# A block of linear attention and a gated MLP on one core: residual of the down phase added in DRAM, two more products by seven, W_down sums moved, the last tile in three parts, a new order

## The chip, the cores and the metric

The kernel runs on one core of a Trainium2 chip. The core has a matrix engine (PE, with its weight loads PEld), a vector engine (DVE), a scalar engine (ACT), GpSimd (POOL) and SyncE (SP), which run their own instruction streams and meet only at semaphores. Matrix products land in PSUM, eight banks of 128 x 512 fp32. SP, ACT and POOL start DMA transfers, which 16 DMA engines carry out. The metric is the device time of one launch in microseconds, the median of several runs: 732.98 us before (732.70 to 734.86, three runs).

## The reference

An adaLN-conditioned block on 2048 rows of width 1024: linear attention with 32 heads, then a gated MLP with 3584 inner columns. Inputs, weights and output are bfloat16.

```python
mod = (silu(c) @ w_mod)                  # six rows of 1024: sa, ca, ga, sb, cb, gb
h = layernorm(x) * (1 + ca) + sa
x = x + ga * A(h, wqkv, wo)              # linear attention
h = layernorm(x) * (1 + cb) + sb
x = x + gb * (gelu(h @ w_gate) * (h @ w_up) @ w_down)
```

The change lies mostly in the last product, `@ w_down`, and in `x + gb * (...)`, the residual.

## The kernel before

**Stages.** `start_phase` and `kvq_phase` make the attention's K, V and Q products; `merge_phase` folds the per-head matrices and Wo into one weight; `wo_phase` multiplies by it, writes the sum x2 (the first residual) to `x2_scr` in DRAM and its normalised form to `xh_scr`. Then the MLP runs in two groups g = 0 and 1 of 1024 rows each: `gate_up(g)` (gate and up products, 14 units of about 12 us) and `down_out(g)` (the product with W_down, gate, residual and store).

**Products by seven.** Large products are cut into 2 x 2 blocks and done with seven block products in place of eight (Winograd's form of Strassen's scheme). In `down_out` the seven products of the outer level are called b11, b21, t0, t1, b22, t2 and t3, by the quarter of W_down, or the sum of quarters, that they read. Each is a product of 512 rows by 1792 by 512 columns. It is done in one of two ways:

- `plain(name, A, out, start)`: W_down's operand is loaded in one DMA of 1792 KB; for each of four row tiles q, 14 matmuls with 512 columns, so 56 matmuls.
- `nested(name, A, S, keep, out)`: by seven once more. Seven operands of 448 KB are loaded; each of the steps g1 to g7 is 14 matmuls with 256 columns, so 98 matmuls. It needs four sums of A's blocks on DVE (`sub_sums`, into the tiles `S`), four sums of W_down's blocks made beforehand (in `u_scr` for b21, b22 and t0, in `v_scr` for b11 and t2), and copies of partial results from PSUM on ACT (`fcopy`).

Before the change, nested are b21, t0 and b22 in both groups, and b11 and t2 in group 1; plain are b11, t1, t2, t3 in group 0 and t1, t3 in group 1.

**W_down's sums.** t0 to t3 are made in DRAM or through SBUF: `wd_moves` lets POOL issue copies and accumulating DMAs (28 in all) from W_down into `t_scr`; `wd_sums` makes, on DVE, t1, t3 and the block sums of `u_scr` in `merge_phase` and `gate_up(0)`. `wd_later(c)`, called in the units 0 to 6 of `gate_up(1)`, loads two rows of b11 and of t2, makes eight sums on DVE and stores them to `v_scr` by POOL.

**Residual.** `rest(half, nh)` loads a 512 KB block of x2 into SBUF on SP's queue; the output functions (`c11_out`, `u2_out`, `c12_out`, `finish`, `c22_quads`, `c21_last`) multiply by the gate row `gbrow`, add that block on DVE, and `store` sends 256 KB blocks to the output, by POOL's queue in group 0 and by ACT's in group 1. All DVE additions of this kind go through the helper `tt_op`, so they all carry line 789.

**The end.** In group 1 the last product is t3 (`plain` with `c21_last`), row tiles in the order 0 to 3; the last tile is done in two parts of 256 columns, which lie in the same PSUM bank.

**Order.** Nothing is issued as it is called: `Plan` records every operation with its dependences and estimated cost, sweeps the list forwards and backwards to give each a due time (`order`), and `refine` then moves the instructions of each engine by hand-fixed shifts from the tables `SHIFTS`, one table for each of PE, DVE, ACT, POOL and SP. Each engine issues in its own fixed order.

**Memory.** SBUF is laid out by hand. `W_AT[g][name]` gives the slots of 3.5 KB per partition that the operands of W_down use. The tiles `x2_ring` at 207 to 219 KB take the x blocks that `wo_tile` adds in `wo_phase`; `early_r`, `early_t`, `early_u` at the same place serve `wd_sums(0)` and `wd_sums(1)`.

```python
        def store(xt, half, nh, lo, hi, c=slice(0, NW)):
            r = (2 * g + half) * TG
            (ac if last else gp).dma_start(
                out=o_dram[r + lo * P:r + hi * P, nh * NW:(nh + 1) * NW][:, c].rearrange("(q p) n -> p q n", p=P),
                in_=xt[:, lo:hi, c])
```

Of the kernel before, what the change touches and what calls it, by code (L numbers as in the profile page):

```python
# [509 lines left out]
def kernel(  # L510
# [839 lines left out]
    def wd_moves(seen_of, n):  # L1350


        if not wd_todo:
            return
# [185 lines left out]
    def merge_phase(stages):  # L1540
# [4 lines left out]
        for i, stage in enumerate(stages):  # L1545
# [20 lines left out]
            if i >= 6:  # L1566
                wp_step(wp.pop(0))
# [636 lines left out]
```

## Time and profile before

The profiled execution took 735.55 us by the clock of the runs; its span, from the first to the last instruction, is 733.5 us, so 2.05 us lie around it. The median of the runs is 2.57 us lower than this execution. Shares are of the span.

| | before |
|---|---|
| median of the runs | 732.98 us |
| profiled execution, its span | 735.55 us, 733.5 us |
| PE busy | 723.0 us (99%), 4352 matmuls |
| DVE busy | 652.4 us (89%), 1470 instructions |
| ACT busy | 455.6 us (62%) |
| POOL busy | 101.5 us (14%) |
| mean granted TensorE clock | 0.995 |
| DMA | 159.26 MB, mean 217 GB/s |

By stage (start and end in us of the span): start, K, V and Q 0 to about 150; merge about 150 to 186; Wo products 186 to 240; `gate_up(0)` 240 to about 404; `down_out(0)` about 404 to 480; `gate_up(1)` about 480 to 648; `down_out(1)` about 648 to the end. The stages overlap by some us, since an engine begins the next as soon as its operands are there.

A profile line names the source line, the engine, the operation, what it writes and reads (`mem` is the SBUF tile, `psum` the PSUM tile, `us`, `vs`, `ts`, `x2s` the DRAM scratch tensors), how many there were, and then busy time and the mean duration of one. A mean duration of a matmul includes its way through the array; the spacing of matmuls that follow each other is read from a block of them instead.

### The profile page before, as it was taken

To read this page: it belongs to the slowest core of one execution; us is meant where nothing else is said; L and a number is where in the kernel's file an instruction comes from. 1 tells how busy PE (TensorE), PEld (TensorE's weight loads), DVE (VectorE), ACT (ScalarE), POOL (GpSimd) and SP (SyncE) were. 2 spreads that over 40 slices of the span, in tenths; PEclk is the share of its full clock that TensorE was granted. 3 is DMA by queue.
4 is the path that set the end of the run, shared out by engine and by line. 5 is a ranking of instruction groups with operands and counts; after the bars stand their busy time and mean duration, and the time that the engine had idled before them with its cause. 6 is when DMAs were issued, how large, how long until landed. Compare 5 with 4: busy or idle time off the path is not lost.

```text
span 733.5 us, 12117 instructions
## 1 busy us (share of the span) xinstructions
PE 723.0 (99%) x4352; PEld 405.7 (55%) x4365; DVE 652.4 (89%) x1470; ACT 455.6 (62%) x829; POOL 101.5 (14%) x174
## 2 busy tenths in 40 slices
PE   7999999999999999999999999999999999999997
PEld 3444545444444555555555677445555555568774
DVE  5699988797699999998998698978898999999998
ACT  4485656579687799999877722027676776743110
POOL 2143616010031014120200000010000100000000
PEclk8999999999999999999999999999999999999999
DMA  9868659988999777765776999554343544489982
GB/s 310 293 195 231 178 130 164 292 304 248 285 241 256 255 242 214 236 213 187 245 203 189 266 315 286 190 173 162 121 133 126 188 157 140 141 234 314 268 271 87
DMA packets 160988, 159.26 MB, mean 217 GB/s; under 512 B 34208, under 2 KB 140448, under 8 KB 160288
## 3 DMA queue, kind: packets, MB, share of 16 engines
q1 hardware_dynamic: 143568, 122.30, 55.6%
q0 software_dynamic: 14848, 33.82, 15.3%
q10 hardware_dynamic: 2512, 2.36, 1.0%
q8 instruction: 34, 0.56, 0.3%
q14 instruction: 26, 0.21, 0.1%
HBM read 122.42 MB, written 36.04 MB: 216 GB/s over the span
## 4 chain that ended last, share of the span: by engine, by line
PE 91%; ACT 3%; DMA 2%; DVE 2%; issue 1%; POOL 1%; SPq 0%; DVEq 0%; ACTq 0%
PE psum L1716 33%; PE psum L1977 12%; PE psum L1727 11%; PE psum L1932 10%; PE psum L1157 8%; PE psum L1227 5%; PE psum L1598 3%; PE psum L1534 3%; PE psum L1256 2%; PE psum L924 2%; DVE mem L789 1%; DMA mem<-in_A_x_dram 1%; DMA mem<-in_w_mod_dram 1%; PE psum L1271 1%; ACT mem L1317 0%
## 5 line engine op out<-in xcount | busy, mean ns | idle before, releaser
L789 DVE TENSOR_TENSOR mem<-mem 128x256 f16<-128x256 f16 (+12 forms) x855 | 377.9, 484 | 17.9 <-ACT mem L1094 4.6
L1716 PE MATMUL psum<-mem 128*128 128x512 f16 x1144 | 274.3, 379 | 0.1
L1094 ACT ACTIVATE mem<-psum 128x512 f32<-128x512 f32 (+3 forms) x318 | 165.0, 552 | 138.3 <-DVE mem L789 38.2
L789 DVE TENSOR_TENSOR mem<-psum,mem 128x512 f16<-128x512 f32 (+5 forms) x213 | 159.3, 756 | 34.3 <-ACT mem L1094 5.6
L1716 PEld LDWEIGHTS <-mem 128*128 128x128 f16 (+1 forms) x1144 | 111.8, 98 | 101.8 <-issue 0.3
L1727 PE MATMUL psum<-mem 128*128 128x256 f16 x742 | 107.4, 272 | 0.0
L1727 PEld LDWEIGHTS <-mem 128*128 128x128 f16 (+1 forms) x742 | 72.4, 98 | 43.1 <-issue 0.8
L1977 PE MATMUL psum<-mem 128*128 128x256 f16 (+1 forms) x784 | 88.2, 273 | 0.0
L1977 PEld LDWEIGHTS <-mem 128*128 128x128 f16 x784 | 76.7, 98 | 11.9
L1932 PE MATMUL psum<-mem 128*128 128x512 f16 (+2 forms) x348 | 75.2, 370 | 0.6 <-DVE mem L789 0.5
L1157 PE MATMUL psum<-mem 128*128 128x512 f16 (+1 forms) x274 | 62.2, 379 | 0.3
L1932 PEld LDWEIGHTS <-mem 128*128 128x128 f16 x350 | 34.2, 98 | 36.0 <-issue 0.7
L789 DVE TENSOR_TENSOR psum<-psum,mem 128x256 f32<-128x256 f32 x106 | 44.6, 427 | 8.7 <-ACT mem L1094 8.3
L1227 PE MATMUL psum<-mem 128*128 128x512 f16 x224 | 51.7, 379 | 0.0
L1772 ACT ACTIVATE psum<-psum 128x512 f32<-128x512 f32 x56 | 32.7, 586 | 30.4 <-DVE mem L789 21.9
L1157 PEld LDWEIGHTS <-mem 128*128 128x128 f16 x280 | 27.2, 98 | 31.6 <-DVE mem L1053 0.2
L1791 ACT ACTIVATE mem<-psum 128x512 f16<-128x512 f32 x56 | 33.1, 598 | 9.5 <-PE psum L1716 9.2
L1227 PEld LDWEIGHTS <-mem 128*128 128x128 f16 (+1 forms) x224 | 21.6, 98 | 25.3 <-issue 0.6
L1801 ACT ACTIVATE mem<-mem 128x512 f16<-128x512 f16 x56 | 34.7, 629 | 0.0
L1256 PE MATMUL psum<-mem 128*128 128x512 bf16 x123 | 29.0, 380 | 1.4 <-DVE mem L1029 0.8
L1335 POOL DMA_DIRECT2D ts<-in_B_w_down_dram x28 | 27.6, 1179 | 5.3 <-DMA ts<-in_B_w_down_dram 5.2
L1534 PE MATMUL psum<-mem 128*128 128x512 f16 x128 | 28.3, 379 | 0.0
(144 smaller groups left out, 574.6 us busy)
## 6 DMA issues: line engine op xcount, KB each, us to landing
mem<-in_B_w_gate_dram SPq DMA_DIRECT2D x14, 1024.0 KB, 5.3
mem<-in_B_w_up_dram SPq DMA_DIRECT2D x14, 1024.0 KB, 6.3
mem<-in_w_mod_dram SPq DMA_DIRECT2D x24, 512.0 KB, 6.8
mem<-us SPq DMA_DIRECT2D x24, 448.0 KB, 6.8
mem<-ts SPq DMA_DIRECT2D x5, 1792.0 KB, 6.7
ts<-in_B_w_down_dram POOLq DMA_DIRECT2D x28, 256.0 KB, 4.8
mem<-in_B_w_down_dram SPq DMA_DIRECT2D x15, 448.0 KB, 6.9
mem<-in_A_x_dram SPq DMA_DIRECT2D x23, 256.0 KB, 5.4
```

What stands on the lines that cost most here:

```text
L789: ve.tensor_tensor(out=out, in0=a, in1=b, op=op)
L1094: ac.activation(out=t, in_=ps, func=AF.Copy)
L1157: te.matmul(ps, lhsT=A[:, k, i * P:(i + 1) * P], rhs=B[:, k, :], start=(start and k == 0), stop=(k == KH - 1), skip_group_check=True)
L1227: te.matmul(o, lhsT=W[:, k, (j0 + i) * P:(j0 + i + 1) * P], rhs=h_form(a, k), start=(start and k == 0), stop=(k == KH - 1), skip_group_che ...
L1256: te.matmul(ps, lhsT=hr1[b][:, k, tl * P:(tl + 1) * P], rhs=Wk[:, k, n * NW:(n + 1) * NW], start=(k == 0), stop=(k == KD - 1))
L1534: te.matmul(psw[:, half, :], lhsT=pqT[b][:, g, tl * P:(tl + 1) * P], rhs=Wp[:, g, half * NW:(half + 1) * NW], start=(g == 0), stop=(g == K ...
L1716: te.matmul(ps, lhsT=a[:, k, e, :], rhs=b[:, k, :], start=(start and k == 0), stop=(k == KH - 1), skip_group_check=True)
L1727: te.matmul(ps, lhsT=self.x[a][:, k, :], rhs=self.y[y][:, k, :], start=(start and k == 0), stop=(k == KH // 2 - 1), skip_group_check=True)
L1791: ac.activation(out=o, in_=ps, func=AF.Gelu_apprx_tanh)
L1801: ac.activation(out=o, in_=o, func=AF.Gelu_apprx_tanh)
L1932: te.matmul(psm[:, q, c], lhsT=A[:, i, q * P:(q + 1) * P], rhs=wt[:, i, c], start=(start and i == 0), stop=(i == NPR - 1), skip_group_chec ...
L1977: te.matmul(ps[:, q, :], lhsT=a[:, k, q * P:(q + 1) * P], rhs=y[:, k, :], start=(start and q == 0 and k == 0), stop=(k == NPR // 2 - 1), s ...
```

## The change

1. **Residual.** `rest` and the DVE additions of x2 go, in all of group 0 and in half 0 of group 1. A new `added(half, nh)` gives a tile of the gated product in fp16, and its `send` adds 256 KB of it onto `x2_scr` in DRAM with an accumulating DMA on POOL's queue. When a half (512 rows) has been sent whole, one DMA copies its 1 MB from `x2_scr` to the output. Half 1 of group 1 stays as it was: loaded, added on DVE, stored by ACT's queue.
2. **Two more products by seven.** b11 in group 0 and t1 in group 1 go from `plain` to `nested`. With them come four sums of A11 each, the output functions `p1_quads` (now in both groups) and `u2_quads` (new), new tiles (`sub_c`), new slots in `W_AT`, and another interleaving of the steps (for example n1[5] and n1[6] behind n2[0] and n2[1]). In group 1 the copies that seed PSUM banks 0 to 3 move from `p1_quads` to `u2_quads`.
3. **W_down's sums.** `v_scr` holds sums for b11, t2 and now t1. Those of b11 are made in `merge_phase` (`wd_first`, stages 4 to 10) through SBUF tiles at 207 to 215 KB. Those of t2 and t1 are made wholly in DRAM: 16 copies and accumulating DMAs of 448 KB, two in each of the units 1 to 8 of `gate_up(1)`. `wd_later`'s loads, DVE sums and stores go.
4. **The last tile.** t3 of group 1 runs its row tiles in the order 2, 3, 0, 1; the last is done in three parts of 256, 128 and 128 columns, the second and third in banks 2 and 3, into which ACT copies the partial sums first.
5. **Order.** All five tables of `SHIFTS` are new. PE has 4463 instructions in them (4365 before), DVE 1429 (1457), ACT 810 (804), POOL 184 (153), SP 225 (226).

```diff
...
+    f32_ring.i = 2
...
-    wdv_rings = {"b11": Ring(207, [2, NW], BF16, 2), "t2": Ring(211, [2, NW], F16, 2)}
-    wdw_ring = Ring(215, [2, 4, HB], F16, 1)
+    first_r, first_v = Ring(207, [2, NW], BF16, 2), Ring(211, [4, HB], F16, 2)
...
-    sub_c = [at(a, [NPR // 2, HB], F16) for a in (207, 210.5, 214, 203)]
+    sub_c = [[at(a, [NPR // 2, HB], F16) for a in o] for o in ((215, 166, 170, 203), (207, 210.5, 214, 203))]
...
-    def wd_later(c):
...
+    def wd_first(c):
+
+        raw, v = first_r(), first_v()
+        plan.ahead = 60000
+        sy.dma_start(out=raw, in_=wd_full["b11"][:, 2 * c:2 * c + 2, :])
+        plan.ahead = 14000
+        q11, q12, q21, q22 = (raw[:, e, h * HB:(h + 1) * HB] for e in range(2) for h in range(2))
+        o0, o1, o2, o3 = (v[:, f, :] for f in range(4))
+        for out, a, b in ((o0, q11, q12), (o2, q12, q22), (o1, o0, q22), (o3, o1, q21)):
+            tt_op(out, a, b, ALU.add)
+        gp.dma_start(out=v_scr[:, c, 0], in_=v)
+
+    def wd_later():
...
+            todo.append([(o0, w[:, 0, 0], 0), (o2, w[:, 0, 1], 0), (o0, w[:, 0, 1], 1), (o2, w[:, 1, 1], 1),
+                         (o1, o0, 0), (o1, w[:, 1, 1], 1), (o3, o1, 0), (o3, w[:, 1, 0], 1)])
...
+            if 4 <= i < 4 + NPR // 2:
+                wd_first(i - 4)
...
-            if g and n < NPR // 2:
-                fill += wd_later(n)
+            if g and n == 0:
+                wd_todo.extend(wd_later())
+            if g and n:
+                wd_moves(w["s1"][:, 0, 0, 0:1], 2)
...
-    W_AT = [{"b11": 0, "b21": (4, 5, 6, 7, 8, 9, 10), "t0": (11, 12, 13, 0, 1, 2, 3), "t1": 4,
-             "b22": (14, 11, 12, 13, 8, 9, 10), "t2": 0, "t3": 11},
+    W_AT = [{"b11": (1, 2, 3, 4, 0, 5, 6), "b21": (7, 8, 9, 10, 11, 12, 13), "t0": (1, 2, 3, 4, 0, 5, 6), "t1": 11,
+             "b22": (7, 8, 9, 10, 4, 5, 6), "t2": 0, "t3": 11},
...
-             "t1": 11, "b22": (7, 8, 9, 0, 1, 2, 3), "t2": (4, 15, 16, 17, 18, 5, 10), "t3": 11}]
+             "t1": (11, 12, 13, 14, 7, 8, 9), "b22": (0, 1, 2, 3, 4, 15, 16),
+             "t2": (17, 18, 5, 6, 11, 12, 13), "t3": 7}]
...
+        def added(half, nh):
+
+            xt = acc_ring()
+
+            def send(lo, hi):
+                gp.dma_start(
+                    out=x2_scr[2 * g + half][lo * P:hi * P, nh * NW:(nh + 1) * NW].rearrange("(q p) n -> p q n", p=P),
+                    in_=xt[:, lo:hi], accum_op=ALU.add)
+                sent[half] += hi - lo
+                if sent[half] == 2 * TT:
+                    r = (2 * g + half) * TG
+                    gp.dma_start(out=o_dram[r:r + TG, :], in_=x2_scr[2 * g + half])
+            return xt, send
...
+            for q in (2, 3, 0, 1) if end else range(TT):
+                parts = [(0, HB, q), (HB, 3 * P, 2), (3 * P, NW, 3)] if end and q == 1 else [(0, NW, q)]
+                for lo, hi, b in parts:
+                    c = slice(lo, hi)
+                    if b != q:
+                        steps.append(lambda c=c, b=b, q=q: ac.activation(out=psm[:, b, c], in_=psm[:, q, c], func=AF.Copy))
...
-        def u2_out(xt):
-            def out(q, ps, c):
-                t = w12[:, q, :]
-                d = p5v[:, q, :] if last else t
-                tt_op(d, p5v[:, q, :], ps, ALU.subtract)
-                tt_op(t, d, gbrow[:, NW:D], ALU.mult)
-                tt_op(t, t, xt[:, q, :], ALU.add)
-            return out
...
+        def u2_out(q, ps, c):
+            t = w12[:, q, :]
+            tt_op(t, p5v[:, q, :], ps, ALU.subtract)
+            tt_op(t, t, gbrow[:, NW:D], ALU.mult)
+
+        def u2_quads(r, c, ps, sb, op):
+            u = quad(p1v, r, c)
+            if sb is not None:
+                tt_op(sb, ps, sb, op)
+                ps = sb
+            tt_op(u, ps, u, ALU.add)
+            if (r, c) in ((1, 0), (0, 1)):
+                rows = slice(2 * r, 2 * r + 2)
+                for q in (2 * r, 2 * r + 1):
+                    ac.activation(out=psm[:, q, :], in_=p1v[:, q, :], func=AF.Copy)
+                tt_op(p5v[:, rows], p5v[:, rows], p1v[:, rows], ALU.subtract)
+                tt_op(w12[:, rows], p5v[:, rows], gbrow[:, None, NW:D].to_broadcast((P, 2, NW)), ALU.mult)
...
-        if last:
-            sub_sums(A11, sub_c[:3], sub_c[3], [slice(0, 4), slice(4, NPR // 2 - 1), slice(NPR // 2 - 1, NPR // 2)])
-            run(*nested("b11", A11, sub_c[:3], sub_c[3], p1_quads))
-        else:
-            run(*plain("b11", A11, p1_out, True))
+        sub_sums(A11, S[:3], S[3], [slice(0, 4), slice(4, NPR // 2 - 1), slice(NPR // 2 - 1, NPR // 2)])
+        n1 = nested("b11", A11, S[:3], S[3], p1_quads)
+        run(*n1[:5])
...
+        if last:
+            sub_sums(A11, S[:3], None, [slice(0, NPR // 2)])
+            n6 = nested("t1", A11, S[:3], None, u2_quads)
+            run(n6[0], n5[5], n6[1], n5[6], *n6[2:5])
...
-            run(*plain("t3", A22, c21_last(x1), False))
+            m8 = plain("t3", A22, c21_last(x1), False)
+            run(m8[0], n7[5], m8[2], n7[6], m8[1], *m8[3:])
...
```

More of the change, by code (lines that the diff above doesn't have):

```diff
@@ L713 @@
     yi_at = [{"b11": at(174, [4, KH // 2, HB], F16), "t1": at(215, [4, KH // 2, HB], F16)},
-             {"b11": at(144, [4, KH // 2, HB], F16), "t1": at(148, [3, KH // 2, HB], F16)}]
+             {"b11": at(183, [4, KH // 2, HB], F16),
+              "t1": [at(o, [KH // 2, HB], F16) for o in (187, 188, 26)]}]
     INNER = (("b11", "t1"), ("b11", "t1"))
@@ L724 @@
     xio_ring.slots += Ring(203, [TT, NW], BF16, 1).slots
+    acc_ring = Ring(183, [TT, NW], F16, 1)
+    acc_ring.slots += Ring(203, [TT, NW], F16, 1).slots
     EARLY = 2
@@ L768 @@
     u_scr = scr_pool.tile([P, NPR // 2, 3, 4, HB], F16, name="us", tag="us")
-    v_scr = scr_pool.tile([P, NPR // 2, 2, 4, HB], F16, name="vs", tag="vs")
+    v_scr = scr_pool.tile([P, NPR // 2, 3, 4, HB], F16, name="vs", tag="vs")
     def load_table():
@@ L1340 @@
     NESTED = ("b21", "b22", "t0")
-    LATER = ("b11", "t2")
+    LATER = ("b11", "t2", "t1")
     def wd_quarter(name, kh, h):
@@ L1707, in rows_inner @@
                                   for h in range(2) for c in range(2))
-            t1, t2, t4 = (yi_at[g][name][:, i] for i in range(3))
-            t3 = y12 if (g, name) == (1, "t1") else yi_at[g][name][:, 3]
+            yi = yi_at[g][name]
+            yi = yi if isinstance(yi, list) else [yi[:, i] for i in range(4)]
+            t1, t2, t4 = yi[:3]
+            t3 = y12 if (g, name) == (1, "t1") else yi[3]
             for out, a, b in ((t1, y12, y11), (t2, y22, t1), (t3, y22, y12), (t4, y21, t2)):
@@ L1920, in store @@
             r = (2 * g + half) * TG
-            (ac if last else gp).dma_start(
+            ac.dma_start(
                 out=o_dram[r + lo * P:r + hi * P, nh * NW:(nh + 1) * NW][:, c].rearrange("(q p) n -> p q n", p=P),
@@ L1928, in plain, with mm @@
             sy.dma_start(out=wt, in_=wd_full[name])
-            def mm(q, c):
+            def mm(b, q, c):
                 for i in range(NPR):
-                    te.matmul(psm[:, q, c], lhsT=A[:, i, q * P:(q + 1) * P], rhs=wt[:, i, c],
+                    te.matmul(psm[:, b, c], lhsT=A[:, i, q * P:(q + 1) * P], rhs=wt[:, i, c],
                               start=(start and i == 0), stop=(i == NPR - 1), skip_group_check=True)
             steps = []
-            for q in range(TT):
-                parts = 2 if last and name == "t3" and q == TT - 1 else 1
-                for n in range(parts):
-                    c = slice(n * NW // parts, (n + 1) * NW // parts)
-                    steps += [lambda q=q, c=c: mm(q, c), lambda q=q, c=c: out(q, psm[:, q, c], c)]
+            end = last and name == "t3"
+            for q in (2, 3, 0, 1) if end else range(TT):
[4 more added lines that the diff above has]
+                        steps.append(lambda c=c, b=b, q=q: ac.activation(out=psm[:, b, c], in_=psm[:, q, c], func=AF.Copy))
+                steps += [f for lo, hi, b in parts for c in (slice(lo, hi),)
+                          for f in (lambda q=q, b=b, c=c: mm(b, q, c), lambda q=q, b=b, c=c: out(q, psm[:, b, c], c))]
             return steps
@@ L2028, in f16_pair, with c11_out @@
             return c0_ring().rearrange("p (q n) -> p q n", q=2)
-        def p1_out(q, ps, c):
-            ac.activation(out=p1v[:, q, :], in_=ps, func=AF.Copy)
-        def c11_out(xt):
+        def c11_out(xt, send):
             def out(r, c, ps, sb, op):
@@ L2040, in out @@
                     tt_op(t, sb, quad(p1v, r, c), ALU.add)
-                tt_op(t, t, gate2(0, c), ALU.mult)
-                tt_op(quad(xt, r, c), t, quad(xt, r, c), ALU.add)
+                tt_op(quad(xt, r, c), t, gate2(0, c), ALU.mult)
                 if (r, c) in ((1, 0), (0, 1)):
-                    store(xt, 0, 0, 2 * r, 2 * r + 2)
+                    send(2 * r, 2 * r + 2)
             return out
@@ L2114, in c21_last, with c21_out @@
             return out
-        def c21_out(xt):
+        def c21_out(xt, send):
             def out(q, ps, c):
-                finish(xt, 1, 0, q, ps, None, None, c)
-                if last:
-                    store(xt, 1, 0, q, q + 1, c)
-                elif q % 2:
-                    store(xt, 1, 0, q - 1, q + 1)
+                finish(xt, 0, q, ps, None)
+                if q % 2:
+                    send(q - 1, q + 1)
             return out
@@ L2137, in down_out @@
                 f()
-        xt = rest(0, 0)
-        n2 = nested("b21", A12, sub_b[:3], sub_b[3], c11_out(xt))
+        n2 = nested("b21", A12, sub_b[:3], sub_b[3], c11_out(*added(0, 0)))
+        run(n2[0], n1[5], n2[1], n1[6])
         for c in range(NPR // NC):
@@ L2143, in down_out @@
         sub_sums(A1x, sub_a, None, [slice(0, NPR // 2)])
-        run(*n2[:5])
+        run(*n2[2:5])
         n5 = nested("t0", A1x, sub_a, None, p5_out)
@@ L2151, in down_out @@
         run(*n5[2:5])
-        xo = rest(0, 1)
-        m6 = plain("t1", A11, u2_out(xo), False)
-        run(m6[4], n5[5], m6[5], m6[6], n5[6], *m6[7:], *m6[:4])
-        if not last:
+        if last:
+            sub_sums(A11, S[:3], None, [slice(0, NPR // 2)])
+            n6 = nested("t1", A11, S[:3], None, u2_quads)
+            run(n6[0], n5[5], n6[1], n5[6], *n6[2:5])
+        else:
+            m6 = plain("t1", A11, u2_out, False)
+            run(m6[4], n5[5], m6[5], m6[6], n5[6], *m6[7:], *m6[:4])
             for f in h2_steps:
                 f()
-        n3 = nested("b22", A12, sub_b[:3], None, c12_out(xo))
-        run(*n3[:5])
+        n3 = nested("b22", A12, sub_b[:3], None, c12_out(*added(0, 1)))
+        if last:
+            run(n3[0], n6[5], n6[6], *n3[1:5])
+        else:
+            run(*n3[:5])
         if last:
```

52 lines of the change are left out of this document (24 added, 28 removed), and 359 rows, old and new, of the table SHIFTS.

## The prediction

> **What bounds the kernel now.** I read the page's parts 1 and 2 first, then the chain in order of time, the table by stages, and the order of instructions at the end and at the change from merge to Wo.
>
> ```profile
> span 733.5 us, 12117 instructions
> PE 723.0 (99%) x4352; PEld 405.7 (55%) x4365; DVE 652.4 (89%) x1470; ACT 455.6 (62%) x829; POOL 101.5 (14%) x174
> PE   7999999999999999999999999999999999999997
> ```
>
> PE is idle for 10.5 us in all: some 5 before 45 us, 3.5 behind the last matmul, 0.85 at 198 us, 0.52 at 728 us. So shorter PE work shortens the run, as long as nothing takes PE's place. The price of PE work is read from unbroken blocks of the chain, since a matmul's own duration (379 and 273 ns) includes its way through the array:
>
> ```profile
> 443.40 10.70 PE psum L1977 x98
> 460.18 15.11 PE psum L1932 x70
> ```
>
> A 256-column matmul takes 10.70/98 = 109.2 ns, a 512-column one 15.11/70 = 215.9 ns. The table by stages (PE, PEld, DVE, ACT, POOL, then clock, DMA share, GB/s) shows who is close behind PE:
>
> ```profile
> 404.00:485.00 81.00, 80.89 (x524) 51.24 (x524) 71.02 (x129) 22.81 (x39) 3.46 (x5) 1.00 0.86 263
> 485.00:655.00 170.00, 170.00 (x994) 96.81 (x992) 153.29 (x402) 115.25 (x247) 6.17 (x10) 1.00 0.47 149
> 655.00:734.00 79.00, 74.49 (x580) 56.50 (x578) 73.03 (x121) 11.47 (x20) 0.00 (x0) 1.00 0.79 237
> ```
>
> In the last down phase DVE is busy for 73.03 us beside PE's 74.49: it is all but a second bound there. In the first it has 10 us to spare. The end and the change to the Wo products, from the order of instructions in time (start, length, engine, line, in brackets the idle time before and who ended it), with one piece of the chain among them:
>
> ```profile
> 728.32 1.69 PE L1932 MATMUL psum<-mem 128*128 128x256 f16 x14 [0.52 <-DVE mem L789]
> 730.04 0.42 DVE L789 TENSOR_TENSOR mem<-psum,mem 128x256 f16<-128x256 f32 x1
> 730.50 0.43 DVE L789 TENSOR_TENSOR mem<-mem 128x256 bf16<-128x256 f16 x1
> ...
> 188.47 7.95 DMA mem<-in_A_x_dram
> ...
> 196.51 1.23 DVE L789 TENSOR_TENSOR mem<-psum,mem 128x1024 bf16<-128x1024 f32 x1 [4.94 <-DMA mem<-in_A_x_dram]
> ```
>
> PE waits 0.52 us for DVE to read the first half of the last tile out of the bank that the second half goes to. At 196.5 us the first Wo tile's addition waits 4.94 us for its x block, and PE then stands 0.85 us at 198.4.
>
> **The change part by part.** The sum is made against the profiled 735.55 us (span 733.5 and 2.05 around it); the median of the runs is 2.57 lower, and I take the sum off that.
>
> *Two products by seven.* A plain product is 56 x 0.2159 = 12.09 us, a nested one 98 x 0.1092 = 10.70. Two of them: -2.78 us, all on PE's path. The row of the weight loads (98 ns each) fits into the 109 ns slot, and the 129-column matmuls of line 1271 come every 57.5 ns (24 in 1.38 us), so short matmuls keep their rate. The Trainium skill ("TensorE: Matmul & The Clock Gate", Back-to-back issue gap) speaks against this part: it gives 131 ns for 512 columns and 81 for 128 as the sustained spacing of load-and-multiply pairs in a real kernel. By that, with an estimate of 98 ns at 256 between the two, a plain product would be 7.3 us and a nested one 9.6, so the change would cost 4.5 us; the trace's 215.9 and 57.5 contradict both of its figures.
>
> *First down phase, DVE and ACT.* Added: 12 sums of A11 (4 each of 1024, 512 and 256 columns at 685, 419 and 285 ns: 5.6 us), 3 additions at 685 (2.1 us). Gone: 16 residual additions (4 at 685 in u2, 12 at 515: 8.9 us). Net -1.3 us beside 10 us of slack; ACT gets 4 more copies (2.4 us) where it is 28% busy. What is late instead: the sums lie in tiles that unit 13 still uses (215, 166, 170 KB), so none is ahead of time as in group 1, and PE's third step needs them 3 us into the product. And five of b21's operands now lie in slots (9 to 13) that unit 13 or the loads of h2 hold to the end; a step takes 1.53 us and its 448 KB at the 305 GB/s seen at 430 to 440 us takes 1.5. Bounds: 0 (group 1 runs b11, b21 and t0 this way at 655 to 680 without a gap) and 3 us (a load landing in 6.8 us against some 4 us of other steps in front of it). I take 0.3, near the lower row.
>
> *Last down phase, DVE.* t1 nested: 4 sums of 1792 columns (4.35 us), 7 additions at 685 (4.8), 4 operations on 1024 fp32 columns at 1.22 (4.9), against 12 x 0.685 = 8.2 before: +5.8. Four residual additions of c11 go: -2.1. The last tile's extra part: +0.3. Net +4.0 us, while PE's time shrinks by 1.39 + 0.52. From 655 to 730 us DVE was busy 72.2 of 75; now 76.2 would have to fit into 73.1. Cover: the 56 sums of `wd_later` (56 x 0.285 = 16 us) leave gate_up(1), where the last of them ran at 630 us, so work that was late there can go before 655: two line-1910 and three line-1911 operations and one sum, 3.8 us. Need: 72.4, leaving 0.7 us for idle moments; there were 2.8, of which one was 1.32 behind ACT. DVE with a longer backlog idles less; if half of the other 1.5 stays, nothing is missing. Bounds: 0, and 76.2 + 2.8 - 73.1 = 5.9 (nothing moves). I take 0.2.
>
> *Last tile.* The third part is in a bank of its own: the 0.52 us wait goes. Behind the last matmul DVE has two operations on 128 columns, about 0.3 each by the step from 512 to 256 (685 to 425), in place of 0.42 and 0.43 with their gap (0.92): -0.3. 28 matmuls of 128 at 57.5 ns for 14 of 256: +0.08. Two ACT copies and one more store on ACT's queue lie beside PE (ACT idle since 714.9). Bounds of the tail: 0 to -0.5. From the store's issue to the end (2.5 us) nothing changes.
>
> *Accumulating DMAs.* POOL issues 12 of them (256 KB) and three 1 MB copies; SP loses six loads of 512 KB. The row for what they cost is line 1335, copies and accumulating DMAs of 256 KB: 1.18 us of POOL, landing after 4.8 (at most 11.7). POOL has nothing else to do in the down phases (3.46 us in 81) and none behind it in group 1 but `wd_moves`, whose 16 moves are done by unit 8 of 14, 40 us before SP's first load of their result (635.9). The last chain: c12's last output leaves DVE some 17 us before PE's end; send (11.7 at worst) and copy (11.7 again) would end about 2.5 us behind the last store, typically (4.8 + 1.2, then 6 to 9 for 1 MB) 5 us before it. DMA share at 715 to 725 us was 0.01. I take 0; bounds 0 and +2.5.
>
> *wd_first in merge.* 28 sums of 285 ns (8 us of DVE, with 3 to 5 us free of every 10 at 160 to 200 us), 7 SP loads and 7 POOL stores of 256 KB where the DMA share is already 0.87 to 1.03. The x blocks of Wo tiles 0 to 3 use the same SBUF and stand behind them. Seven chunks through two buffers: 3.5 turns of a landing (x loads: 5.4 median) plus 1.14 of DVE = 23 us, against 29.5 from POOL's last early store (153.7, landing 5.3) to 188.47. I take 0; bounds -0.85 (the wait at 198 goes) and +7 (below).
>
> *Other order.* New tables can move the 5 us of idle PE before 45 us and the 0.85; before shows nothing of it, so -1 to +1, taken as 0.
>
> Sum: -2.78 + 0.3 + 0.2 - 0.52 - 0.3 + 0.08 = -3.0 us. 735.55 becomes 732.5, the median 732.98 becomes 730.0.
>
> **The rivals.**
> - *DVE becomes the bound of the last phase.* For: 98% busy, +4.0 us of work. Against: the 16 us freed ahead of it. If only half of the 3.8 us moves and idle moments stay at 1.5, it lacks 76.2 - 1.9 + 1.5 - 73.1 = 2.7, and the time is 732.98 - 3.0 + 2.5 = 732.5: no difference.
> - *The x blocks come late (slower).* For: tile 0's addition already waits for its block, and PE stands right behind. Against: 6 us of slack by median landings. It decides from a turn of 29.5/3.5 = 8.4 us on. With landings of 9.3 us (the wqkv loads on the same queue) it is 10.4 x 3.5 = 36.5, 7.0 us late, each of them PE's: 737.
> - *The new order gains more.* The 0.85 and half of the idle 3 us between 8 and 45 us gone: 727.6. For: these waits hang on order alone; against: they are the start's loads, which no table makes faster.
> - *Short matmuls cost more than they save.* Weight loads as the slot: +4.5 instead of -2.8, so 737.3. The rows above speak against it everywhere. It is the rule named above.
>
> **How the numbers follow.** Forecast 0.53 (its own range 728.6 to 731.6: some 0.42 beyond 0.3% and 0.11 within); better order 0.17; DVE bound 0.14; late x blocks 0.14 (0.11 slower, 0.03 within, where the lateness only eats the gain); short matmuls 0.02. 0.3% is 2.2 us, about what a measurement of this kernel can tell from no change: faster is below 730.8, slower above 735.2. So faster 0.59, same 0.28, slower 0.13. The predicted time is 730.0. The range goes down to 727.0 (the better order) and up to 734.6 (DVE's bound and the upper ends of 3 and 2.5 us); it leaves out the later x blocks, the short matmuls and the best of the orders, under 0.2.
>
> **What would show it.** Right: blocks of 98 matmuls of line 1977's successor in 10.7 us for b11 in group 0 and t1 in group 1; PE without idle time from 404 to the end; no wait before the last 14 matmuls; two 128-column DVE operations at the end; the last x2 copy landed before the last store. Wrong: PE waiting for DVE (line 789) in the last 70 us; SP's x loads behind POOL's `vs` stores and PE idle near 190 to 200; PE waiting for `vs` or `us` loads near 415 to 435; matmuls of 256 columns slower than 109 ns.

## The result and the profile after

The change makes the kernel slower. Its median is 737.03 us (11 runs, 735.81 to 739.36), that of the kernel before, run beside it, 734.48 us (11 runs, 732.70 to 735.65). The ratio is 1.0043, with a 95% interval of 1.0029 to 1.0056. Forecast were 730.0 us and a range up to 734.6. The base of the forecast was low too: it took the median of three runs, 732.98, and all later series of the kernel before gave 734.45 to 734.71. Against that base the forecast was -3.0 us and the result +2.55 between the medians (+3.2 by the ratio), so some 5.5 to 6.2 us have to be explained.

The profiled execution of the changed kernel took 738.93 us, 1.9 above its median. The page of the changed kernel (parts 1, 3 and 6):

```profile
span 737.1 us, 12351 instructions
PE 721.4 (98%) x4463; PEld 413.0 (56%) x4463; DVE 652.3 (88%) x1442; ACT 460.2 (62%) x838; POOL 132.0 (18%) x205
...
q0 software_dynamic: 25440, 43.52, 23.7%
```

PE has less to do and still ends later. What has grown is POOL's DMA queue, q0: 25440 packets, where the kernel before had 14848. The waits of PE from 404 us on, in the same execution (microseconds in all, times, longest), and the table by stages (PE, PEld, DVE, ACT, POOL, clock, DMA share, GB/s):

```profile
PE psum L1740 <- DVE psum L789: 3.0, 2, 2.2
PE psum L1966 <- DMA mem<-ts: 1.0, 1, 1.0
```

```profile
490.00:560.00 70.00, 67.31 (x395) 38.41 (x394) 55.19 (x138) 47.98 (x103) 18.32 (x20) 1.00 0.74 179
430.00:440.00 10.00, 9.02 (x71) 6.79 (x70) 9.96 (x17) 3.30 (x6) 0.00 (x0) 1.00 0.89 291
640.00:730.00 90.00, 90.00 (x733) 71.18 (x731) 85.94 (x144) 25.22 (x49) 5.97 (x6) 1.00 0.97 266
```

Where I had expected trouble, in the last down phase, PE is busy without a break (90.00 of 90). It stands still where I had expected nothing: 2.7 us in the second gate/up phase and 1.0 us in the first down phase. Both are places where a DMA is late. The order of instructions around the longest wait:

```profile
520.49 2.45 POOL L1335 DMA_DIRECT2D vs<-ts  x2 [5.50 <-DMA vs<-ts]
521.96 2.25 POOL L1936 DMA_DIRECT2D x2s<-mem  x1
523.24 0.37 SPq L1688 DMA_DIRECT2D mem<-in_B_w_up_dram  x1
526.95 0.99 POOL L1335 DMA_DIRECT2D vs<-ts  x1 [2.75 <-DVE mem L789]
535.19 0.29 DVE L789 TENSOR_TENSOR mem<-mem 128x256 f16<-128x256 bf16 x1 [2.66 <-DMA mem<-in_B_w_up_dram]
537.15 0.38 PE L1740 MATMUL psum<-mem 128*128 128x256 f16 x2 [2.24 <-DVE psum L789]
```

Just ahead of the 1 MB load of "up" weights at 523.24 POOL has issued two W_down moves and one accumulating send, and behind it another move. The chain of the execution gives the load 11.93 us (the median of such loads is 5.1 to 5.4). DVE's sums of these weights wait for it, the work behind them on DVE waits too, and PE waits 2.24 us for DVE. In the DMA records the load's first packet comes 3.54 us after its issue, where the load issued at 510.67 has it after 1.04 us; from then until 534 it shares the engines with POOL's packets.

The end, in the order of instructions:

```profile
723.65 0.42 ACTq L1955 DMA_DIRECT2D out_dram<-mem  x1
724.07 0.53 POOL L1942 DMA_DIRECT2D out_dram<-x2s  x1 [4.59 <-DMA x2s<-mem]
728.30 6.42 ACTq L1955 DMA_DIRECT2D out_dram<-mem  x7
731.75 0.29 DVE L789 TENSOR_TENSOR mem<-mem 128x128 bf16<-128x128 f16 x1
```

The last copy of a block of x2 to the output (1 MB) is issued at 724.07 and takes 8.2 us, so it lands when the last stores are issued. One of those stores (line 1955) takes 3.52 us to issue, and the span ends 5.8 us after the last matmul, against 3.5 before.

### The profile page after: what moved, and what is told of

Its sections match the earlier page's. It is cut to its first block, busy times and chain, and to the rows that moved or that the text cites. A ratio compares the mean times of both kernels' runs of the same rounds, so it can differ in the third digit from the quotient of the medians.

```text
span 737.1 us, 12351 instructions
## 1 busy us (share of the span) xinstructions
PE 721.4 (98%) x4463; PEld 413.0 (56%) x4463; DVE 652.3 (88%) x1442; ACT 460.2 (62%) x838; POOL 132.0 (18%) x205
## 3 DMA queue, kind: packets, MB, share of 16 engines
q0 software_dynamic: 25440, 43.52, 23.7%
## 4 chain that ended last, share of the span: by engine, by line
PE 87%; DMA 6%; DVE 4%; issue 1%; POOL 1%; ACT 0%; SPq 0%; DVEq 0%
PE psum L1729 31%; PE psum L2015 13%; PE psum L1740 10%; PE psum L1157 7%; PE psum L1227 6%; PE psum L1966 5%; PE psum L1256 3%; PE psum L1609 3%; PE psum L1543 3%; DVE mem L789 3%; PE psum L924 2%; DMA mem<-in_B_w_up_dram 2%; DMA mem<-ts 1%; DMA mem<-in_B_w_gate_dram 1%; DMA mem<-in_B_w_down_dram 1%; DMA mem<-in_w_mod_dram 1%
## 5 line engine op out<-in xcount | busy, mean ns | idle before, releaser
L789 DVE TENSOR_TENSOR mem<-mem 128x256 f16<-128x256 f16 (+14 forms) x823 | 374.4, 498 | 16.3 <-DMA mem<-in_B_w_up_dram 3.8
L1094 ACT ACTIVATE mem<-psum 128x512 f32<-128x512 f32 (+3 forms) x324 | 170.0, 554 | 116.5 <-PE psum L2015 41.7
L789 DVE TENSOR_TENSOR mem<-psum,mem 128x512 f16<-128x512 f32 (+5 forms) x221 | 164.7, 752 | 31.7 <-ACT mem L1094 11.7
L2015 PE MATMUL psum<-mem 128*128 128x256 f16 (+1 forms) x980 | 108.6, 273 | 0.0
L1740 PE MATMUL psum<-mem 128*128 128x256 f16 x742 | 105.1, 273 | 3.5 <-DVE psum L789 3.5
L2015 PEld LDWEIGHTS <-mem 128*128 128x128 f16 x980 | 95.9, 98 | 13.0
L1936 POOL DMA_DIRECT2D x2s<-mem x12 | 15.6, 1496 | 210.9 <-DVE mem L789 207.2
L1966 PE MATMUL psum<-mem 128*128 128x512 f16 (+2 forms) x252 | 49.6, 355 | 1.0 <-DMA mem<-ts 1.0
L1157 PEld LDWEIGHTS <-mem 128*128 128x128 f16 x280 | 26.8, 98 | 32.8 <-DVE mem L1053 1.3
L1966 PEld LDWEIGHTS <-mem 128*128 128x128 f16 x252 | 23.5, 98 | 25.1 <-issue 1.2
```

The costliest lines, as they stand in the source:

```text
L789: ve.tensor_tensor(out=out, in0=a, in1=b, op=op)
L1094: ac.activation(out=t, in_=ps, func=AF.Copy)
L1157: te.matmul(ps, lhsT=A[:, k, i * P:(i + 1) * P], rhs=B[:, k, :], start=(start and k == 0), stop=(k == KH - 1), skip_group_check=True)
L1740: te.matmul(ps, lhsT=self.x[a][:, k, :], rhs=self.y[y][:, k, :], start=(start and k == 0), stop=(k == KH // 2 - 1), skip_group_check=True)
L1966: te.matmul(psm[:, b, c], lhsT=A[:, i, q * P:(q + 1) * P], rhs=wt[:, i, c], start=(start and i == 0), stop=(i == NPR - 1), skip_group_chec ...
L2015: te.matmul(ps[:, q, :], lhsT=a[:, k, q * P:(q + 1) * P], rhs=y[:, k, :], start=(start and q == 0 and k == 0), stop=(k == NPR // 2 - 1), s ...
```

## The experiments

All edits are to the changed kernel. They are made after the planner has laid out its order (an operation is skipped, moved in one engine's order, or given other operands when it is issued), so that PE, DVE and ACT keep the order of the changed kernel, except in the two runs without tables. "Tail" below is the time from the end of the last matmul to the end of the span.

**Smaller pieces for the copies to the output.** As one contiguous block, each 1 MB copy goes in 16 pieces of 64 KB.

```diff
-gp.dma_start(out=o_dram[r:r + TG, :], in_=x2_scr[2 * g + half])
+gp.dma_start(out=o_dram[r:r + TG, :].rearrange("(q p) n -> p q n", p=P),
+             in_=x2_scr[2 * g + half].rearrange("(q p) n -> p q n", p=P))
```

> The three copies of a finished block of rows to the output are given in pieces of 2 KB (one row) instead of 16 pieces of 64 KB; nothing else changes. Theory A (a 64 KB piece keeps its DMA engine for 2.8 to 4.5 us, the issue of ACT's last stores stands behind it for 3.52 us): the longest issue of a store falls below 0.7 us, the tail behind the last matmul from 5.8 us to some 3.5, the time from 737.0 to some 734.7 (ratio to the kernel before 1.000). Rival B (what counts is the megabyte that still moves at the end, in whatever pieces, or the order of the last stores): tail 5 to 6 us, time 737 (ratio 1.0035).

Measured: 737.93 us, ratio 1.0048 (1.0033 to 1.0062). The last stores by line (minimum, median, maximum of an issue in ns), first in the changed kernel and then here:

```profile
L1955 ACTq DMA_DIRECT2D out_dram<-mem x8: 388/416/3521, 723.6 to 734.3; - x8
```

```profile
L1955 ACTq DMA_DIRECT2D out_dram<-mem x8: 351/414/479, 723.0 to 731.6; - x8
```

The stall of the store's issue is gone, as theory A says, but the time is as long as before: the tail is still 4.7 us, within the 3.8 to 5.9 us of the five runs in this document that keep 64 KB pieces at the end. So the large pieces do stall the issue, and it is not they that set the time. Theory A falls as an explanation of the time; rival B stands.

**The copy of group 0's second half earlier.**

```diff
 POOL's order: ... W_down moves,
+  copy of x2 block 1 to the output
   four sends of group 1,
-  copy of x2 block 1 to the output,
   copy of x2 block 2 to the output
```

> Only the copy of group 0's second half to the output is moved ahead in POOL's order, from 718 us (right before the last four sends) to behind the last W_down move near 585 us. Theory A (the last copy's own 64 KB pieces stall the store): the last copy is still under way at 728 to 732 us, so the tail stays 5 to 6 us and the time 736.5 to 737. Rival C (it takes two copies, one behind the other, to make the last one late): the last one lands before 731, tail 3.5 us, time 734.7. If the moved copy hits a gate/up weight load, up to 2 us come on top near 585 us.

Measured: 738.57 us (734.48 to 739.85), ratio 1.0047 (1.0031 to 1.0063); the moved copy starts at 584.43, the tail is 4.2 us. That is neither the 5 to 6 us of theory A nor the 3.5 of C: one copy at the end still lengthens the tail, and how much the second one adds a single execution doesn't show. The profiled execution showed something else, in the table by stages around the late load, where the clock is the third number from the end:

```profile
537.00:539.00 2.00, 0.92 (x5) 0.53 (x5) 2.00 (x7) 0.38 (x1) 0.00 (x0) 0.90 0.75 220
539.00:541.00 2.00, 2.00 (x9) 0.93 (x8) 1.93 (x5) 1.65 (x3) 0.65 (x2) 0.50 0.87 304
541.00:543.00 2.00, 2.00 (x8) 0.84 (x7) 2.00 (x5) 0.02 (x1) 1.47 (x1) 0.75 0.00 1
```

After PE's wait of 2.0 us the granted clock is 0.50 for 3.4 us (by the three rows, 0.4 + 2.0 + 1.0): PE is "busy", with 9 matmuls in the middle row where the same stretch of the changed kernel has 11. So one late load can cost more than its wait, and whether it does differs from one execution to the next; the last section says what decides it.

**Without the W_down moves.**

```diff
 gate_up(1):
-  16 moves of W_down quarters (line 1335), two per unit
 last down phase, t2 and t1: operands t1, t0, t2, t3
-  from v_scr[:, :, 1] and v_scr[:, :, 2]
+  from v_scr[:, :, 0]
```

> The 16 moves of W_down quarters in the second gate/up phase are left out (the nested products t2 and t1 of the last down phase then read the sums of b11 in their place, the same bytes from the same scratch tensor, so those two products are computed from other weights). Theory D (the moves' 512 B pieces take the DMA engines from the gate/up weight loads): no load of 1 MB lands later than 6 us, PE has no gap from 490 to 655 us (3.3 us in the profiled execution of the changed kernel), time 737.0 - 2 to 3.3, so 733.7 to 735. Rival E (the late weight load comes from the order on SP or DVE, the moves ride in free DMA time): gaps near 534 and 559 us stay, time 737.

Measured: 734.45 us (12 runs, 731.97 to 737.53), ratio 1.0002 (0.9989 to 1.0016). The second gate/up phase and the only wait of PE from 404 us on:

```profile
490.00:560.00 70.00, 70.00 (x413) 40.05 (x411) 57.67 (x143) 49.05 (x108) 5.22 (x9) 1.00 0.37 107
```

```profile
PE psum L1966 <- DMA mem<-ts: 0.7, 1, 0.7
```

PE, DVE and SP have the same instructions in the same order as in the changed kernel, and both gaps of the second gate/up phase are gone. Between the two ratios to the kernel before lie 0.41%, or 3.0 us (2.6 between the medians): this is the largest part of the miss, and it is the moves. Rival E falls. What the run doesn't tell is whether moves must cost that, or only moves that meet a load. The next two runs ask this.

**Pairs of moves behind the loads.**

```diff
 in each unit n from 1 to 8:
-  wait for a sum of unit n's weights, then two moves
+  wait until the weights of unit n + 2, loaded in this unit, have landed, then two moves
 POOL's order:
+  group 0's sends and first copy ahead of all moves
```

> The same 16 moves, two per unit as in the program's text, but each pair starts only when the weight load issued in that unit has landed (POOL's small gate copy reads the landed weights instead of a sum of the unit before), and group 0's last sends and copy stand ahead of them. Theory D (it is the collision that costs, not the moves as such): loads land in 5 to 6 us, no gap of PE from 490 to 655 us, time as without the moves, 733.7 to 735. Rival F (the moves cost by their bytes wherever they lie, or push the W_down loads of the last phase back): gaps or late loads remain, time 736 to 737.

Measured: 739.38 us (6 runs, 737.27 to 743.19), ratio 1.0071 (1.0048 to 1.0094), worse than the change itself. A pair, its issue, the next load and PE's waits from 404 us on; and the clock behind the longest of them:

```profile
534.35 2.99 POOL L1335 DMA_DIRECT2D vs<-ts  x2 [0.50 <-issue]
...
537.84 0.37 SPq L1688 DMA_DIRECT2D mem<-in_B_w_gate_dram  x1
```

```profile
PE psum L1740 <- DVE psum L789: 3.2, 2, 2.3
PE psum L1740 <- DVE mem L789: 1.3, 1, 1.3
PE psum L1966 <- DMA mem<-ts: 0.8, 1, 0.8
```

```profile
564.00:566.00 2.00, 2.00 (x7) 0.80 (x6) 1.96 (x5) 1.69 (x4) 0.00 (x0) 0.60 0.75 283
566.00:568.00 2.00, 2.00 (x6) 0.70 (x5) 0.83 (x3) 0.00 (x0) 0.00 (x0) 0.54 0.80 215
```

A unit is 12 us long. The load takes 5 of them or more, the pair is issued 7 to 11 us after the load, and the packets of this pair go on until 11 us behind its issue: the next load is then already issued (537.84), and has its first packet 3.2 us later. Theory D as I had put it falls, since a wait for the landing does not keep the two apart; F holds for pairs. Not for all of them, though. Four of the eight pairs are two plain copies (112 packets of 4096 B each): the four loads issued behind those had their first packets after 1.01 to 1.04 us. The other four are two accumulating moves (896 packets of 512 B each): the loads behind those had them after 3.05 to 3.63 us. The pairs of copies were also through 1.1 to 1.6 us behind the load's issue, those of accumulating moves only 5.7 to 9.5 us behind it, so this run does not tell the size of the packets from the time that a pair lasts.

**One move per unit.** As in the run before, a small copy on POOL that reads the landed weights does the waiting; now it stands ahead of each single move.

```diff
-  in units 1 to 8: two moves
+  in units 0 to 11: when the weights of unit n + 2 have landed, one move (t1's first)
+  behind the last weight load: the last four
```

> The same 16 moves again, but one per unit: move k starts when the weight load that unit k issues has landed (twelve units), those of product t1 first, and the last four after the last weight load; group 0's sends and copy stand ahead of them. In the run with pairs behind the loads a load issued while a pair was still under way got its first packets only 2.4 to 3.7 us later. Theory D' (a move and a weight load have to take turns on the DMA engines; a pair, some 5 us of packets at about 350 of 512 B a microsecond plus 3 us until the first one, does not fit between a landing and the next load, a single one does): loads land in 5 to 6 us, no gap of PE from 490 to 655 us, time as without the moves, 734 to 735. Rival F (moves cost by their bytes): as in the changed kernel, 737. Rival H (the last four moves, now at 625 to 640 us, hit the W_down loads of the last phase): gaps move to 650 to 700 us, 736 to 738.

Measured: 735.01 us (6 runs, 732.36 to 737.35), ratio 1.0005 (0.9982 to 1.0028). The same stretches of the second gate/up phase:

```profile
490.00:560.00 70.00, 70.00 (x411) 40.01 (x410) 57.95 (x143) 49.60 (x108) 11.18 (x15) 1.00 0.60 151
560.00:640.00 80.00, 80.00 (x465) 45.23 (x464) 71.91 (x175) 56.21 (x121) 11.61 (x14) 1.00 0.60 149
```

All 16 moves are there, with DMA share 0.60, and PE never waits in the gate/up phase (its one wait from 404 us on is the 0.7 us for the t1 load). F falls for single moves, H does not come about, and D' stands: what costs is a load that meets a move. The interval of six runs leaves room for some 1.7 us either way; that the gaps are gone is seen in the trace. The share of the DMA engines was no sign of it. From 490 to 640 us it was 0.62 in the changed kernel, 0.61 with pairs behind the loads and 0.60 here, and PE was busy for 147.02, 145.43 and 150.00 of the 150 us.

**Sends straight onto the output, and the plain t1 load in halves.**

```diff
+copies of x2 blocks 1 and 2 to the output: behind the last gate/up weight load (623 us)
-group 1's sends: accumulate onto x2_scr[2], then copy it to the output
+group 1's sends: accumulate onto the output's rows
 plain("t1") of group 0:
-sy.dma_start(out=wt, in_=wd_full[name])
+for i in (0, 7):
+    sy.dma_start(out=wt[:, i:i + 7], in_=wd_full[name][:, i:i + 7])
```

> Two edits at places that the trace tells apart. First: the last sends of group 1 are added straight onto the output; x2's copy to the output is made before them, near 626 us, behind the last gate/up weight load, together with that of group 0's second half, so no megabyte moves after 718 us. Theory B (that megabyte delays the last stores): the span ends 3.5 to 3.7 us after the last matmul, as before the change, where the runs with the copy at the end show 4.0 to 5.8; -0.5 to -2.3 us. Rival I (the longer tail comes from ACT issuing four stores for the last tile instead of two): 4 to 4.5 us stay. Second: the plain t1 load of 1.79 MB in group 0 is issued as two halves, so that the first half need not wait for the last slot to come free. Theory J (PE's 1.0 us at 436 us is that load, 8.5 us from issue to landing): gap gone, -1.0. Rival: the halves queue behind the same DMA work and the gap stays. Sum by theories B and J: 737.0 - 1.0 - 0.5 to 2.3 = 733.7 to 735.5; the collision near 534 us stays.

Measured: 735.40 us (6 runs, 733.99 to 736.52), ratio 1.0009 (0.9991 to 1.0027). The stretch of the t1 load, the issues at the end, and PE's longest remaining wait:

```profile
430.00:440.00 10.00, 10.00 (x80) 7.63 (x79) 9.96 (x16) 3.08 (x6) 0.00 (x0) 1.00 0.99 297
```

```profile
714.05 2.41 POOL L1936 DMA_DIRECT2D out_dram<-mem  x2 [18.81 <-DVE mem L789]
```

```profile
PE psum L1740 <- DVE psum L789: 1.8, 1, 1.8
```

Theory J holds: 10.00 of 10 us in place of 9.02. Theory B holds: with nothing copied at the end the tail is 3.6 us, with the same four stores on ACT's queue for the last tile, so rival I falls. The collision near 534 us is still there, as it should be.

**Without the tables of shifts.** Two kernels in the planner's own order:

```diff
-for e, text in SHIFTS.items():
+for e, text in {}.items():
```

> The kernel before with its written tables of shifts taken out (the planner's own order). It serves as the base for the next one. The planner's own order was never timed here: I expect 740 to 760 us.

> The changed kernel without its tables, to be set against the one before without its tables. Theory D (what the change costs is in its DMAs, not in its new tables): the difference of the two is that of the tabled kernels, +1 to +4 us. Rival G (the new tables are the worse ones, the structure itself gains the 3 us that PE's work lost): -1 to -4 us.

Measured: 767.14 us (4 runs) for the kernel before, 786.94 (4 runs) for the changed one, so +19.8 us where I had expected +1 to +4 or -1 to -4. Neither theory had this. The largest waits of the same kind, before and after, with their lines' numbers in each:

```profile
PE psum L1727 <- DVE psum L789: 5.1, 7, 2.5
```

```profile
PE psum L1740 <- DVE psum L789: 14.4, 7, 5.1
```

Four of the latter, of 2.3 to 5.1 us, lie between 540 and 630 us, in the second gate/up phase, where the moves are. Of the 22 us between the two profiled spans (787.5 and 765.5), 14.5 are idle time of PE and 7.5 are longer busy time (738.2 against 730.7, though the products by seven make the work less), at a mean granted clock of 0.976 against 0.989. So in the planner's order the change costs far more than with the new tables (14.4 us of this wait are 3.0 there). That these four waits are the moves is argued from their place; no run without tables left the moves out. That the new orders of PE, DVE and ACT are not what makes the change slow is shown by the last run below, which keeps all three and is faster than the kernel before.

**The three edits together.** In this run the first two units carried the two copies of x2, and six moves were left for the time behind the last weight load.

> The three edits that helped, in one kernel that computes the whole reference: one W_down move per unit behind that unit's weight load (here the first two units carry the two copies of x2 to the output, the next ten a move each, the last six moves come behind the last weight load), group 1's last sends added straight onto the output, and the plain t1 load of group 0 in two halves. If the three costs are separate: 737.0 - 2.0 - 1.0 - 0.6 to 1.6 = 732.4 to 733.4, ratio to the kernel before 0.997 to 0.999; the last matmul near 728 us, the span's end 3.5 to 3.7 us later, no gap above 0.2 us from 404 us to the end. Rival: the six moves at 625 to 645 us hit the W_down loads of the last phase and give it back: gaps between 650 and 700 us, 734 to 736.

Measured: 737.65 us (6 runs), ratio 1.0049 (1.0033 to 1.0065): the rival. The latest move, PE's only wait from 404 us on, and the table by stages there:

```profile
655.08 1.48 POOL L1335 DMA_DIRECT2D vs<-ts  x1 [7.15 <-DMA vs<-vs]
```

```profile
PE psum L2015 <- DMA mem<-in_B_w_down_dram: 3.0, 1, 3.0
```

```profile
688.00:692.00 4.00, 1.04 (x9) 0.65 (x7) 4.00 (x6) 0.60 (x1) 1.26 (x2) 0.91 0.97 259
692.00:694.00 2.00, 2.00 (x12) 1.38 (x10) 1.52 (x2) 0.00 (x0) 1.23 (x1) 0.50 0.81 199
```

Each edit did its part (no wait in the gate/up phase or at 436 us, tail 3.6 us), but now a W_down load is late: the one that SP issues at 684.46, where the last run below, whose last move starts at 646.73, issues it at 679.86. PE waited 3.0 us at 688 and then ran at half the clock for 3.4. That the late moves push these loads back is argued from where they lie, as the DMA engines have little slack there (DMA share 0.97 in the first row, up to 1.18 by 698 us); no run moved only them.

**No moves, sends straight onto the output, t1 in halves.**

> The same without any of the 16 moves (t2 and t1 of the last phase read b11's sums in their place, so those products are computed from other weights): what the change would be worth with its matmuls and its DVE work as they are and none of its three DMA costs. From the run without moves, 734.45 - 1.0 - 0.6 to 1.6: 731.9 to 732.9. If it comes out at 730 as I forecast for the change, the DMA costs were the whole error; what it stays above that is the new order's share (0.8 us of PE at 87 us, some 0.7 at 322 to 369 us).

Measured: 731.75 us (11 runs, 731.11 to 735.24), ratio 0.9969 (0.9954 to 0.9983). With its DMA costs taken out the change is faster by 2.3 us (ratio) to 2.7 us (medians), where I had forecast 3.0. By the ratios the moves are worth 3.0 us and the two edits for the copies and the t1 load 2.5; both together here are worth 5.4, so the costs add up.

**x2 kept in the output.**

```diff
+stores of x2, its later loads for group 1 and the accumulating sends, blocks 0 to 2:
+  on the output's rows in place of x2_scr[0] to x2_scr[2]
-the three copies to the output
+W_down moves: one per unit, as above; t1 load of group 0 in halves
```

> In the run with the three edits together the copies of x2 had pushed W_down moves past 655 us, and PE waited 3.0 us for a W_down load at 688. Here the copies are gone altogether: x2's first three blocks are kept in the output itself from the Wo stage on (the stores of x2, its later loads for group 1 and the accumulating sends all name the output's rows), so nothing is copied. The moves are one per unit from the first unit on, as in the run that had only this edit, the last four behind the last weight load; the plain t1 load of group 0 is in two halves. If the moves cost nothing once they take turns with the loads, and without the copies: the time of the run without any moves, 731.75, plus at most 1.0 = 731.8 to 732.8, ratio to the kernel before 0.997 to 0.998, no gap of PE above 0.4 us from 404 us to the end, 3.5 to 3.7 us behind the last matmul. Rival: the late moves still push the W_down loads past 680 us: one gap of 1 to 3 us between 650 and 700 us, 733 to 735.5.

Measured: 732.47 us (6 runs, 731.16 to 733.23), kernel before 734.71 us, ratio 0.9963 (0.9950 to 0.9977). This version beats both kernels, with all 16 moves in it; against the run with the three edits together it has no copies to the output and four moves behind the last weight load in place of six, and no run tells the two apart. Its page, the second gate/up phase and the last stores:

```profile
span 731.2 us, 12350 instructions
```

```profile
490.00:560.00 70.00, 70.00 (x412) 40.12 (x411) 57.93 (x144) 49.13 (x107) 10.83 (x14) 1.00 0.56 134
560.00:640.00 80.00, 80.00 (x465) 45.14 (x463) 71.53 (x174) 56.41 (x121) 12.27 (x15) 1.00 0.61 153
```

```profile
L1955 ACTq DMA_DIRECT2D out_dram<-mem x8: 351/415/480, 719.9 to 728.4; - x8
```

The trace shows no wait of PE from 404 us to the end, and the tail is 3.6 us.

## Why the prediction was wrong

- *Two products by seven, -2.78 us: right.* In the changed kernel's chain a block of 518 matmuls takes 56.56 us, 109.2 ns each, as forecast; the rival of dearer short matmuls did not come.
- *Last down phase, DVE, +0.2: right.* PE is busy in every one of the last 90 us before 730, so DVE never became the bound.
- *First down phase, +0.3: wrong in place and size.* I had priced a late load of b21's operands. The load that came late is the plain t1's: 1792 KB, issued at 428.75 when its last slot came free, 8.51 us to landing, 1.0 us of PE. It is within the bounds given (0 to 3). In halves it cost nothing.
- *Accumulating DMAs, taken as 0: wrong, within its bound of +2.5.* The failed sentence is that the last copy would end 5 us before the last store. It was issued at 724.07 and took 8.2 us. The tails of 3.8 to 5.9 us in the six runs with a copy at the end, and 3.6 in the four without, put this at 0.2 to 2.3 us. I had looked at when the last output leaves DVE, not at the send that must land (4.59 us of POOL's wait) before the copy can start.
- *The moves of gate_up(1): the step that failed.* "POOL has nothing else to do", I wrote, and checked that the moves would be done 40 us before their result is loaded. That is true, and beside the point. I costed the moved work on its own queue and against its own reader, and not against the other transfers in flight: the 1 MB weight loads that PE needs every 12 us. The run without moves puts it at 3.0 us, and the run with one move per unit gives nearly all of that back (2.0 between the medians, 2.8 by the ratios).
- *x blocks late: right that they would not be.* The wait of 0.85 us at 198 us is gone; a new one for DVE stands at 192 us, ahead of line 1286, 0.3 us in this execution and up to 0.8 in others. *Last tile:* the wait of 0.52 us went; the shorter tail of -0.3 did not come, 3.6 us without copies against 3.5.
- *Other order, 0: about right.* PE's wait of 0.7 us at 87 us (for ACT, line 1094) is new in every run of the changed order, and 0.5 to 1.5 us near 322 to 369 us in eight of the ten; the first K product starts 0.4 to 2.3 us earlier than in the execution of before, and the last Q product within 1.2 us of it.

So the sum of PE and DVE work was right to within 0.7 us, as the run without DMA costs shows (ratio 0.9969, -2.3 us with an interval of -3.4 to -1.2, against -3.0). What stays above that is of the size of the waits in the last point; no run took them away.

## What to carry to other kernels

Work moved from an engine to a DMA queue is not free because that queue and its issuing engine are idle: ask which transfers are in flight at the same time, and which of them the bound engine waits for. A mean DMA share tells little: over the same phase 0.60 cost PE nothing, 0.61 cost 4.6 us and 0.62 cost 3.0. What decides is whether a move is under way when the load is issued, so give the two turns, one move per gap, and look at the time from issue to first packet. At the end of a kernel, a result that can be added in place needs no copy behind it.

## What the runs showed of the hardware

- A load that meets moves of another queue is late at its start. Without the moves, ten of the twelve loads of 1 MB from 486 us on have their first packet 1.03 to 1.05 us after their issue (the other two, beside late transfers of group 0, 1.15 and 1.88). With the moves it is 1.03 to 3.54 us in the changed kernel and 3.05 to 3.63 us for four loads of the run with pairs. The Trainium skill ("DMA: Bandwidth & Descriptors", Queues, rings and completion order) says that each engine takes turns between the queues it has work for, a packet at a time. The later part of these loads agrees (from 527 to 533 both queues have packets in every microsecond); the empty first 3.5 us do not follow from it, and no run here shows what held them.
- The accumulating moves go in packets of 512 B, which pass at about 350 a microsecond over all engines (65 ns each in the median), so the 896 packets of a 448 KB move take 2.6 us or more (3.4 to 3.7 from first to last, where one ran alone). A plain copy of 448 KB goes in 112 packets of 4096 B, in 1.9 to 2.2 us. Copies of 1 MB in 64 KB pieces stalled the issue of another queue's store for 3.52 us; in 2 KB pieces they did not, for the same time of the whole.
- A wait of PE of 2.0, 2.3 and 3.0 us was followed by 3.4 us of half clock, which cost up to 1.7 us more; waits of 1.8, 2.2 and 2.2 us in other executions were not. The traces show what tells them apart. In each of the 13 the granted clock changes only on a fixed grid of 3.41 us, and what counts is PE's idle time within one slot of that grid, not the length of the wait. From 17 us to the last matmul, all ten slots of full clock with 2.2 us or more of it were followed by a slot of half clock, none of those with 1.9 us or less was, and of three with 1.96 to 1.99 us one was. The wait of 2.24 us in the changed kernel fell into two slots (1.49 and 0.75 us); the one of 1.96 us in the run with the early copy lay in a single one. Whether this scatters the times is not shown: the changed kernel's runs lie 3.6 us apart, but those of the run without moves, whose trace has no wait above 0.7 us, 5.6. The Trainium skill ("TensorE: Matmul & The Clock Gate", HAM oscillation) gives idle gaps above some 3.4 us as the limit; here shorter ones were enough.
